# A fused RWKV-5 attention and ReLU-squared MLP kernel: q k^T in pairs of units, log w spread first, and another order of all steps

## The chip, the cores and the metric

The kernel runs on one core of a Trainium2 chip. Five engines work from their own in-order queues: TensorE (PE, matmuls and transposes), VectorE (DVE), ScalarE (ACT), GpSimd (POOL) and SyncE (SP); here POOL and SP mainly start DMA transfers. The metric is the device time of one launch in microseconds, lower is better; a time is the median of several runs.

## The reference

The first half is a linear-attention recurrence with a per-channel decay `w` and a bonus `u` for the current token; its output, laid out as 3072 tokens by 384 channels, goes through a two-layer MLP whose activation is the square of a ReLU.

```python
# r, k, v: (4, 8, 768, 48); w, u: (8, 48); moe_w_in: (384, 2048); moe_w_out: (2048, 384)
for t in range(S):
    cur = einsum('bhd,bhe->bhde', u[None] * kt, vt)
    y[:, :, t] = einsum('bhd,bhde->bhe', rt, state + cur)
    state = w[None, :, :, None] * state + einsum('bhd,bhe->bhde', kt, vt)
x = y.transpose(0, 2, 1, 3).reshape(B * S, H * D)
out = (maximum(x @ w_in, 0.0) ** 2) @ w_out
```

## The kernel before

The sequence is cut into 6 chunks of 128 tokens; a *unit* is one chunk of one of the 4 batches, so there are 24 units, numbered chunk by chunk. Within a chunk the recurrence becomes matrix products: r is scaled by powers of w and k by inverse powers (`scale`), both are turned so that channels lie on the partitions, and their product, masked to the strictly earlier tokens, weights v. What comes from earlier chunks goes through a state of 48 by 48 per head.

The code is a set of small step functions and one long string, `SCHEDULE`, which lists all steps in program order. Each engine executes its own steps in the order in which they stand there. The numbers behind `@` are the PSUM banks (there are 8) that a step takes. The steps that matter:

- `load:i:kt:SP` loads k (or r, v) of unit i with a DMA started by SP or POOL (192 KB); `win` and `wout` load a quarter of the two weight matrices, cast to bf16, started by POOL (384 KB each, line 274 and line 279).
- At the start, `spread_log` spreads log w over the partitions by a matmul (line 237) from a row that ACT has taken the logarithm of, and `power:0`, `power:1` (ACT, line 241) make the powers `wpos` for r and `wneg` for k from it. `columns` loads w and u again as columns, `spread_columns` transposes them (line 246), `copy_columns` copies them out, and `u_columns` and `end_columns` (POOL) prepare the bonus and the decay over a chunk. `fill` is a matmul whose result nobody reads; it keeps TensorE occupied.
- `scale:i:0` and `scale:i:1` (DVE, line 288) write the scaled r and k. For units 0 to 5 `turn` (TensorE, line 311) and `evict_rk` (ACT) turn them; for units 6 to 23 `turn_dma` does it with one transposing DMA on SP's queue.
- `rk` (DVE) multiplies turned r and k for the bonus. `at:i` (TensorE, line 328) is q k^T of the unit: 8 matmuls of contraction 64 into two banks; `mask:i:o` (DVE, line 336) masks one bank out to SBUF.
- `sums` (lines 344, 349) makes the bonus and the addition to the state, `diag_v`, `state_add`, `state_decay`, `state_cast` use it. `y_mm` (lines 387, 393) forms the attention output, `evict_y` writes it as bf16, and `x_turn`/`evict_x` (units 0 to 5) or `x_dma` (a transposing DMA on SP) turn it.
- `mm1:i:m:s` (line 431) is a piece of the first MLP layer for m units at once (one unit for units 0 to 7, two from 8 on), `relu` (ACT) and `square` (on ACT, line 448, or DVE, line 450, as its last number says) follow. `mm2:i:q` (line 457) is a quarter of the second layer of one unit, `evict_o` and `store` write out; the last unit's second layer is done in two halves (line 472).

Of the kernel before, what the change touches and what calls it, by code (L numbers as in the profile page):

```python
# [22 lines left out]
rk:1 at:1@6,7 cast_v:1 end_columns fill:256@5 at:0@0,1 mask:1:1 fill:256@5 load:6:kt:SP fill:256@5 sums:1@2 mask:1:0
2*fill:256@5 3*fill:256@7 diag_v:1 fill:256@7 load:3:rt:POOL y_mm:1@4 cast_v:0 load:6:rt:SP fill:256@7 scale:2:1
4*fill:256@7 evict_y:1 fill:256@7 win:2:0 4*fill:256@7 mask:0:0 x_turn:1@3 turn:2:1@5 load:4:kt:POOL evict_x:1
sums:0@7 scale:2:0 fill:256@4 evict_rk:2:1 fill:256@4 mask:0:1 fill:256@4 turn:2:0@6 win:3:0 cast_v:2 2*fill:256@3
diag_v:0 fill:256@5 evict_rk:2:0 y_mm:0@4 load:4:rt:POOL fill:256@5 scale:3:1 2*fill:256@5 at:2@0,3 load:8:rt:SP rk:2
mm1:1:1:1@5 mask:2:0 wout:0:0 load:5:kt:POOL sums:2@1 evict_y:0 turn:3:1@6 mask:2:1 x_turn:0@0 evict_rk:3:1
mm1:1:1:0@4 wout:1:0 scale:3:0 evict_x:0 load:4:vt:POOL y_mm:2@3 relu:1:1:1 diag_v:2 turn:3:0@6 mm1:0:1:1@0
evict_rk:3:0 evict_y:2 relu:1:1:0 state_add:1 at:3@5,3 cast_v:3 x_turn:2@6 mm1:0:1:0@4 rk:3 evict_x:2 mask:3:1  # L30
square:1:1:0:1 sums:3@2 mm1:0:1:2@6 mask:3:0 wout:2:0 load:7:rt:SP diag_v:3 mm1:2:1:1@3 relu:0:1:2 state_add:2
load:5:rt:POOL y_mm:3@5 square:0:1:2:1 mm1:2:1:0@6 scale:4:1 relu:0:1:0 mm1:2:1:2@1 evict_y:3 relu:2:1:0 state_add:0
turn:4:1@4 state_cast:1 mm1:1:1:2@5 wout:3:0 square:1:1:1:0 relu:0:1:1 x_turn:3@6 mm1:1:1:3@7 evict_x:3 load:5:vt:POOL
square:0:1:1:0 relu:1:1:2 mm1:0:1:3@0 relu:2:1:1 square:1:1:2:0 mm1:3:1:3@6 square:2:1:1:1 square:2:1:0:0 mm1:3:1:2@5
relu:2:1:2 square:0:1:0:0 mm1:3:1:0@3 evict_rk:4:1 scale:4:0 relu:3:1:3 mm2:2:0@1 relu:3:1:0 square:3:1:3:0 turn:4:0@4
state_cast:0 mm1:3:1:1@6 square:3:1:0:0 mm2:1:0@3 evict_rk:4:0 state_add:3 relu:3:1:2 mm2:1:1 scale:5:1 cast_v:4
square:3:1:2:0 relu:0:1:3 at:4@4,2 load:7:kt:SP mm2:3:0@5 state_cast:2 rk:4 mask:4:1 mm1:2:1:3@0 mask:4:0 sums:4@2
relu:2:1:3 mm2:2:1 scale:5:0 square:2:1:2:0 y_mm:4@4 load:8:kt:SP turn:5:1@0 diag_v:4 mm2:1:2 relu:1:1:3 scale:6:1
load:7:vt:SP square:2:1:3:1 mm2:2:2 evict_y:4 evict_rk:5:1 mm2:2:3 scale:6:0 relu:3:1:1 square:1:1:3:0 turn:5:0@7
turn_dma:6 square:0:1:3:1 mm2:0:0@4 state_add:4 cast_v:5 x_turn:4@0 evict_rk:5:0 mm2:1:3 load:6:vt:SP evict_x:4  # L40
at:5@6,2 state_cast:3 load:9:kt:SP mm1:4:1:1@7 mask:5:0 mm1:4:1:0@0 rk:5 load:9:rt:SP relu:4:1:1 scale:8:0 mm1:4:1:3@6
scale:7:0 relu:4:1:0 mask:5:1 mm1:4:1:2@7 square:3:1:1:1 scale:7:1 sums:5@0 relu:4:1:2 mm2:3:1 state_add:5 turn_dma:7
relu:4:1:3 mm2:3:2 square:4:1:1:1 diag_v:5 y_mm:5@2 scale:8:1 cast_v:7 load:8:vt:SP mm2:3:3 square:4:1:0:1 evict_y:5
turn_dma:8 state_decay:4 cast_v:6 at:6@7,6 mm2:4:0@0 square:4:1:3:1 mask:6:1 evict_o:3 load:11:rt:SP x_turn:5@2 rk:6
mm2:0:1 evict_o:1 square:4:1:2:0 load:10:rt:SP state_cast:4 sums:6@6 mask:6:0 mm2:0:2 evict_x:5 diag_v:6 mm2:4:1
state_add:6 y_mm:6@5 at:7@3,7 evict_y:6 mm1:5:1:3@2 mask:7:1 x_dma:6 mm1:5:1:2@6 rk:7 mask:7:0 mm1:5:1:0@5 relu:5:1:2
load:10:kt:SP scale:9:0 sums:7@7 load:9:vt:SP square:5:1:2:1 scale:9:1 y_mm:7@3 mm1:5:1:1@6 relu:5:1:0 state_add:7
turn_dma:9 relu:5:1:3 mm2:4:2 diag_v:7 cast_v:8 rk:8 mm2:0:3 relu:5:1:1 evict_y:7 square:5:1:0:1 state_decay:5
at:8@5,2 x_dma:7 sums:8@7 square:5:1:1:1 mask:8:0 mm1:6:1:0@6 evict_o:2 mask:8:1 mm1:6:1:1@3 load:11:kt:SP relu:6:1:0
diag_v:8 store:2:POOL load:12:kt:SP mm1:6:1:3@5 scale:10:0 store:1:POOL scale:11:0 y_mm:8@1 store:3:POOL relu:6:1:3  # L50
mm2:5:0@2 scale:10:1 square:6:1:0:1 square:5:1:3:0 mm2:5:1 turn_dma:10 relu:6:1:1 evict_y:8 mm1:6:1:2@6 cast_v:9 rk:9
evict_o:0 x_dma:8 at:9@5,3 state_cast:5 sums:9@1 mask:9:0 mm1:7:1:2@4 square:6:1:1:1 mask:9:1 load:11:vt:SP relu:6:1:2
# [5 lines left out]
load:13:rt:SP mm1:8:2:2@7 relu:8:2:1 mm1:8:2:3@1 cast_v:10 square:8:2:1:0 load:14:kt:SP relu:8:2:2 at:11@4,0 rk:11
cast_v:11 mm1:8:2:7@5 mask:11:1 relu:8:2:3 mm1:8:2:0@7 mask:11:0 square:8:2:3:1 sums:10@0 scale:12:0 relu:8:2:0
sums:11@1 y_mm:11@4 turn_dma:12 relu:8:2:7 diag_v:11 mm1:8:2:6@7 cast_v:12 diag_v:10 y_mm:10@5 evict_y:11 relu:8:2:6  # L60
mm2:6:3 square:8:2:0:0 square:8:2:2:1 x_dma:11 mm1:8:2:5@4 scale:13:1 evict_y:10 mm2:8:0@7 relu:8:2:5 load:15:rt:SP
scale:13:0 mm1:8:2:4@5 x_dma:10 square:8:2:5:1 scale:14:1 mm2:9:0@4 square:8:2:6:1 rk:12 square:8:2:7:1 scale:15:1
mm2:7:2 load:14:rt:SP state_add:11 relu:8:2:4 turn_dma:13 mm2:9:1 square:8:2:4:1 mm2:8:1 evict_o:6 load:15:vt:SP
cast_v:13 mm2:8:2 evict_o:5 store:6:POOL load:16:rt:SP sums:12@5 store:4:POOL at:12@1,3 diag_v:12 mm2:8:3 store:0:POOL
mask:12:1 mm1:10:2:1@2 mask:12:0 mm1:10:2:0@3 scale:15:0 relu:10:2:1 scale:14:0 mm1:10:2:3@1 relu:10:2:0 state_add:10
turn_dma:14 mm1:10:2:6@2 square:10:2:0:1 square:10:2:1:0 mm1:10:2:7@3 relu:10:2:3 state_add:12 turn_dma:15
mm1:10:2:2@0 relu:10:2:7 state_decay:9 relu:10:2:6 state_decay:10 at:13@1,5 state_decay:12 y_mm:12@3 relu:10:2:2
load:16:kt:SP rk:13 mm1:10:2:5@2 state_cast:9 evict_y:12 mm1:10:2:4@0 mask:13:1 x_dma:12 square:10:2:2:1 mask:13:0
mm2:7:3 relu:10:2:5 square:10:2:7:0 square:10:2:3:1 sums:13@3 load:14:vt:SP y_mm:13@5 relu:10:2:4 diag_v:13 mm2:11:0@1
state_cast:10 evict_y:13 mm2:10:0@2 scale:16:0 square:10:2:6:1 x_dma:13 mm2:11:1 rk:15 cast_v:15 state_add:13 mm2:9:2  # L70
evict_o:8 load:17:rt:SP square:10:2:4:1 rk:14 mm2:10:1 store:8:POOL state_decay:11 load:17:kt:SP square:10:2:5:1
store:5:POOL at:15@0,5 state_cast:12 load:16:vt:SP at:14@3,7 mm2:10:2 mask:14:1 load:19:rt:SP state_cast:11 mm2:11:2
mask:15:1 cast_v:14 evict_o:7 mm2:9:3 load:19:kt:SP state_decay:13 mask:15:0 sums:15@7 evict_o:9 scale:16:1
mm1:12:2:0@5 mask:14:0 mm1:12:2:1@6 turn_dma:16 sums:14@0 relu:12:2:1 y_mm:14@4 diag_v:14 mm1:12:2:5@3 evict_y:14
mm1:12:2:2@6 relu:12:2:5 scale:17:0 x_dma:14 mm1:12:2:4@4 relu:12:2:0 scale:17:1 diag_v:15 relu:12:2:2 y_mm:15@3
turn_dma:17 square:12:2:1:0 relu:12:2:4 mm2:11:3 cast_v:16 evict_y:15 mm2:10:3 square:12:2:2:1 square:12:2:0:0
# [465 lines left out]
```

## Time and profile before

| | |
|---|---|
| median of 3 runs | 176.25 us (174.26 to 177.11) |
| the profiled execution | 174.99 us |
| its span, first to last instruction | 173.1 us |
| granted TensorE clock | 1.000 |
| busy VectorE / ScalarE / GpSimd | 132.3 / 125.7 / 29.3 us |
| read from HBM, written | 20.45 MB, 4.72 MB |

The page gives busy time by engine, then 40 equal slices of the span with a digit for the busy share of each, the DMA queues (q1 carries what SP starts, q0 what POOL starts), the chain of work that ended last, and the costliest groups of instructions. A busy time of TensorE comes from modelled ends of pipelined matmuls, so the chain, which counts the time that a piece adds, is the better source for what a matmul costs. Under DMA issues, the last number of a row is the median time from issue to landing.

### The profile page before, as it was taken

What the parts mean: (1) busy time and instruction counts of PE and PEld (TensorE: products, weight loads), DVE (VectorE), ACT (ScalarE), POOL (GpSimd) and SP (SyncE); (2) the same over time, 40 slices, a digit from 0 to 9 for tenths busy, and PEclk for the clock granted to TensorE, in tenths of its full rate; (3) what the DMA queues carried; (4) which work ended last, traced back from release to release, by engine and by line L of the source; (5) the groups of instructions that cost most, each with busy time, mean ns of one, the idle gap of its engine ahead of it and who ended that gap; (6) DMA issues with size and microseconds to landing.
All of it is one profiled execution on the core that took longest, in us unless ns stands there. A gap on an engine that the chain in (4) does not pass through costs nothing.

```text
span 173.1 us, 4810 instructions
## 1 busy us (share of the span) xinstructions
PE 165.4 (96%) x1928; PEld 131.9 (76%) x1928; DVE 132.3 (76%) x289; ACT 125.7 (73%) x261; POOL 29.3 (17%) x61
## 2 busy tenths in 40 slices
...
DMA  5999999999996997999997997997969952122023
GB/s 110 198 207 227 215 240 236 245 172 115 205 172 125 200 207 145 200 202 118 254 183 172 209 160 154 193 157 223 225 100 229 263 140 45 27 68 91 4 99 128
DMA packets 95760, 28.83 MB, mean 167 GB/s; under 512 B 91689, under 2 KB 93738, under 8 KB 95738
## 3 DMA queue, kind: packets, MB, share of 16 engines
...
q8 instruction: 15, 0.25, 0.6%
...
HBM read 20.45 MB, written 4.72 MB: 145 GB/s over the span
## 4 chain that ended last, share of the span: by engine, by line
PE 70%; DMA 16%; DVE 4%; ACT 4%; POOL 2%; issue 1%; SPq 1%; DVEq 0%; ACTq 0%
PE bank L431 30%; PE bank L457 27%; DMA ldr<-in_r_dram 7%; DMA rkT<-rkw 6%; PE bank L328 3%; DMA xT<-yb 2%; ACT gr L439 2%; PE bank L387 2%; PE bank L393 2%; PE bank L472 2%; PE bank L349 2%; DVE rkw L288 2%; PE bank L344 1%; DVE g L450 1%; POOL wend_c L260 1%
## 5 line engine op out<-in xcount | busy, mean ns | idle before, releaser
L439 ACT ACTIVATE gr<-bank 128x512 f32<-128x512 f32 x96 | 54.5, 600 | 25.4 <-PE bank L431 24.8
L431 PE MATMUL bank<-xT,w_in_q 128*128 128x128 bf16 (+1 forms) x768 | 71.0, 246 | 0.5 <-DMA xT<-yb 0.5
L457 PE MATMUL bank<-w_out_q,g 128*128 128x384 bf16 x368 | 67.1, 326 | 0.0
L431 PEld LDWEIGHTS <-w_in_q 128*128 128x128 bf16 x768 | 63.6, 113 | 3.5 <-issue 0.7
L457 PEld LDWEIGHTS <-g 128*128 128x128 bf16 x368 | 34.3, 98 | 18.9
L336 DVE TENSOR_TENSOR am<-bank,smask 128x512 bf16<-128x512 f32 x48 | 31.6, 683 | 5.9 <-PE bank L328 5.0
L450 DVE TENSOR_TENSOR g<-gr 128x512 bf16<-128x512 f32 x41 | 27.3, 685 | 11.2 <-ACT gr L439 10.9
L448 ACT ACTIVATE g<-gr 128x512 bf16<-128x512 f32 x55 | 34.0, 635 | 0.6
...
L378 ACT CAST stb<-st 64x192 bf16<-64x192 f32 x40 | 14.0, 349 | 2.8 <-DVE st L372 2.5
L288 DVE TENSOR_TENSOR rkw<-ldk,wneg 128x384 bf16<-128x384 f32 x24 | 13.2, 552 | 3.3 <-ACT wneg L241 3.1
L358 DVE TENSOR_TENSOR dv<-vb,bank 128x384 f32<-128x384 bf16 x24 | 13.1, 548 | 2.5 <-PE bank L349 1.2
L402 DVE TENSOR_TENSOR yb<-bank,dv 128x384 bf16<-128x384 f32 x24 | 13.3, 554 | 1.9 <-PE bank L393 1.1
L288 DVE TENSOR_TENSOR rkw<-ldr,wpos 128x384 bf16<-128x384 f32 x24 | 12.9, 550 | 1.3 <-DMA ldr<-in_r_dram 1.3
L292 ACT CAST vb<-ldv 128x384 bf16<-128x384 f32 x24 | 12.4, 515 | 2.1 <-DMA ldv<-in_v_dram 2.0
L320 DVE TENSOR_TENSOR rk<-rkT 128x512 bf16<-128x512 bf16 x24 | 10.0, 418 | 4.4 <-DMA rkT<-rkw 2.7
L464 ACT COPY osb<-bank 128x384 f32<-128x384 f32 x23 | 10.7, 480 | 2.0 <-PE bank L457 1.9
L368 DVE TENSOR_TENSOR st<-bank,st 64x192 f32<-64x192 f32 x32 | 11.3, 352 | 0.3
L315 ACT COPY rkT<-bank 128x512 bf16<-128x512 bf16 x12 | 6.8, 588 | 4.8 <-PE bank L311 4.8
L233 PE MATMUL bank<-warm 128*128 128x256 bf16 (+1 forms) x50 | 9.1, 328 | 1.2 <-DVE warm L179 1.2
L328 PEld LDWEIGHTS <-rkT 64*128 64x128 bf16 x192 | 5.8, 94 | 5.2 <-issue 4.5
L328 PE MATMUL bank<-rkT 64*128 64x128 bf16 x192 | 9.1, 218 | 0.4 <-ACT rkT L315 0.2
...
## 6 DMA issues: line engine op xcount, KB each, us to landing
ldv<-in_v_dram SPq DMA_DIRECT2D x22, 192.0 KB, 4.5
ldk<-in_k_dram SPq DMA_DIRECT2D x21, 192.0 KB, 4.2
out_dram<-osb POOLq DMA_DIRECT2D x21, 192.0 KB, 3.3
ldr<-in_r_dram SPq DMA_DIRECT2D x19, 192.0 KB, 3.8
w_in_q<-in_moe_w_in_dram POOLq DMA_DIRECT2D x4, 384.0 KB, 7.3
w_out_q<-in_moe_w_out_dram POOLq DMA_DIRECT2D x4, 384.0 KB, 10.4
ldr<-in_r_dram POOLq DMA_DIRECT2D x5, 192.0 KB, 7.2
ldk<-in_k_dram POOLq DMA_DIRECT2D x3, 192.0 KB, 7.8
```

What stands on the lines that cost most here:

```text
L288: nc.vector.tensor_tensor(t["rkw"][:, x, :, :, :D], pair(src), pair(wx), ALU.mult)
L292: nc.scalar.copy(tiles[i]["vb"], tiles[i]["vt"])
L328: nc.tensor.matmul(out=t["at"][o][:, p, :], lhsT=t["rkT"][sl, 1, p, :], rhs=t["rkT"][sl, 0, p, :], start=True, stop=True,)
L336: nc.vector.tensor_tensor(am, t["at"][o], smask.unsqueeze(1).to_broadcast([C, HP, C]), ALU.mult)
L358: nc.vector.tensor_tensor(t["dv"], t["vb"], t["d"].unsqueeze(2).to_broadcast([C, H, D]), ALU.mult)
L378: nc.scalar.copy(stb[b][sl, :, o * D : (o + 1) * D], st32[b][sl])
L402: nc.vector.tensor_tensor(t["yb"], t["y"], t["dv"].rearrange("p h d -> p (h d)"), ALU.add)
L431: nc.tensor.matmul(out=t["h", s][:, a], lhsT=turned, rhs=chunks[c]["xT"][:, n, b : b + m, :], start=(n == 0), stop=(n == NK - 1),)
L439: nc.scalar.activation(t["gr", s], t["h", s], AF.Relu)
L448: nc.scalar.activation(g, x, AF.Square)
L450: nc.vector.tensor_tensor(g, x, x, ALU.mult)
L457: nc.tensor.matmul(out=t["o"], lhsT=chunks[units[i][0]]["g"][:, f, units[i][1], :], rhs=w_out_q[f // 4][:, f % 4, :], start=(f == 0), stop ...
```

## The change

Three things change, all in the order of the steps; the arithmetic stays the same.

1. A new step `ats:i` runs `at:i` and `at:i + 1` back to back, with four banks at once. For units 8 to 23 every q k^T is now such a pair.
2. At the start, `spread_log` comes behind 9 fills and ahead of `spread_columns`, which now stands behind the first four `turn` steps; before, it came behind 14 fills and was directly followed by `spread_columns`. `power:0` (for r) now precedes `power:1`.
3. The whole `SCHEDULE` is another one: other positions, banks, queues of some loads, and another choice of engine for the squares (50 of 96 on DVE where it was 41). The number of fills goes from 50 to 53.

```diff
+    def ats(i):
+        at(i)
+        at(i + 1)
+
     def mask(i, o):
...
-        at, cast_v, columns, copy_columns, diag_v, end_columns, evict_half, evict_o,
+        at, ats, cast_v, columns, copy_columns, diag_v, end_columns, evict_half, evict_o,
...
-load:1:kt:SP fill:256@7 load:0:kt:SP 2*fill:256@7 load:0:rt:SP 2*fill:256@7 load:1:rt:POOL 2*fill:256@7 load:1:vt:SP
-columns:0 2*fill:256@7 columns:1 fill:256@7 win:1:0 fill:256@7 load:2:kt:SP 2*fill:256@7 load:2:rt:POOL fill:128@7
-spread_log@0 load:0:vt:SP spread_columns@1 power:1 power:0 scale:1:1 2*fill:256@7 scale:0:0 turn:1:1@2 scale:0:1
...
-mm2:6:1 load:12:vt:SP mask:10:1 mm2:7:0@6 load:15:kt:SP state_decay:8 state_decay:6 state_cast:8 mm2:6:2 mask:10:0
...
+load:1:kt:SP fill:256@7 load:0:rt:SP 2*fill:256@7 load:0:kt:SP 2*fill:256@7 load:1:rt:POOL 2*fill:256@7 load:2:kt:SP
+2*fill:256@7 columns:0 columns:1 load:1:vt:POOL spread_log@0 load:2:vt:SP load:2:rt:POOL load:5:rt:SP fill:256@7
+power:0 win:0:0 2*fill:256@7 power:1 fill:256@7 scale:0:0 fill:256@7 load:0:vt:POOL fill:256@7 scale:1:1 2*fill:256@7
+turn:1:1@1 win:1:0 scale:0:1 turn:0:0@2 evict_rk:1:1 load:3:kt:POOL scale:1:0 turn:0:1@3 load:5:kt:SP evict_rk:0:0
...
+x_dma:8 mm1:7:1:2@6 relu:7:1:3 state_add:9 mm2:5:3 evict_o:4 square:7:1:1:0 cast_v:11 load:10:vt:SP mm2:7:0@1
+relu:7:1:2 state_decay:9 load:13:rt:SP rk:10 square:6:1:2:1 mm2:7:1 square:7:1:2:0 load:13:kt:SP evict_o:5 mm2:6:2
...
+square:7:1:3:1 scale:12:1 ats:10@0,5,3,2 turn_dma:12 mm1:8:2:0@6 mask:10:1 mm1:8:2:4@4 mask:11:1 relu:8:2:0
```

The queues at the start, in order. SP before: k1 k0 r0 v1 k2 v0 v2 v3 k6 r6 r8 r7 k7 k8 v7, then the transpose of unit 6; after: k1 r0 k0 k2 v2 r5 k5 r6 k6 k9 k7 k8 r7 r8 v6, then the same transpose. POOL before: r1 win 1, r2, `u_columns`, k3, win 0, `end_columns`, r3, win 2, k4, win 3, r4, wout 0, k5, wout 1, v4, wout 2, r5, wout 3, v5; after: r1 v1 r2, win 0, v0, win 1, k3, win 2, r3, `u_columns`, `end_columns`, win 3, v3, wout 0, r4, wout 1, k4, wout 2, v4, wout 3, v5.

More of the change, by code (lines that the diff above doesn't have):

```diff
@@ L23 @@
[L23 to L52, printed above, removed]
@@ L58 @@
[L58 to L76, printed above, removed]
-x_dma:15 mm1:12:2:7@5 square:12:2:5:1 state_add:15 mm1:12:2:3@6 square:12:2:4:0 load:18:kt:SP mm1:12:2:6@4 relu:12:2:3
@@ new lines @@
+turn:1:0@4 evict_rk:0:1 win:2:0 spread_columns@5 evict_rk:1:0 rk:0 load:3:rt:POOL cast_v:1 rk:1 at:1@6,7 copy_columns
+at:0@0,1 u_columns scale:2:0 fill:256@5 scale:2:1 fill:256@5 end_columns turn:2:0@2 fill:256@5 mask:0:0 turn:2:1@3
+evict_rk:2:0 sums:1@4 mask:0:1 evict_rk:2:1 3*fill:256@5 2*fill:256@2 mask:1:0 at:2@5,0 win:3:0 2*fill:256@3 mask:1:1
+2*fill:256@3 fill:256@6 cast_v:0 load:3:vt:POOL 2*fill:256@6 diag_v:1 fill:256@6 y_mm:1@2 y_mm:0@3 load:6:rt:SP
+sums:0@1 evict_y:1 wout:0:0 2*fill:256@7 rk:2 fill:256@7 load:4:rt:POOL x_turn:1@6 diag_v:0 2*fill:256@7 evict_x:1
@@ new lines @@
+2*fill:256@7 fill:256@2 evict_y:0 fill:256@2 wout:1:0 mm1:1:1:1@7 state_add:0 x_turn:0@2 load:4:kt:POOL mm1:1:1:0@6
+mask:2:1 evict_x:0 relu:1:1:1 state_add:1 mm1:0:1:0@3 relu:1:1:0 mm1:0:1:1@1 mask:2:0 square:1:1:1:1 scale:3:1
+relu:0:1:0 4*fill:256@7 square:1:1:0:0 fill:256@7 cast_v:2 3*fill:256@7 state_cast:1 fill:256@7 square:0:1:0:0
+sums:2@2 wout:2:0 y_mm:2@0 mm1:0:1:2@7 relu:0:1:1 diag_v:2 evict_y:2 mm1:1:1:2@4 load:4:vt:POOL load:6:kt:SP scale:3:0
+x_turn:2@6 turn:3:1@5 state_add:2 evict_x:2 turn:3:0@3 fill:256@0 evict_rk:3:1 fill:256@0 square:0:1:1:0 mm1:2:1:2@1
@@ new lines @@
+evict_rk:3:0 wout:3:0 mm1:2:1:0@0 relu:1:1:2 rk:3 relu:0:1:2 at:3@6,2 load:5:vt:POOL relu:2:1:0 mm1:2:1:1@5 mask:3:1
+cast_v:3 mm1:1:1:3@3 square:2:1:0:0 relu:2:1:1 mask:3:0 mm1:2:1:3@4 square:1:1:2:1 square:2:1:1:1 mm1:0:1:3@7
+scale:4:0 relu:2:1:2 mm2:1:0@0 relu:1:1:3 scale:5:0 sums:3@2 relu:0:1:3 y_mm:3@5 turn:4:0@6 diag_v:3 square:2:1:2:1
+mm2:0:0@1 square:0:1:2:1 evict_y:3 mm2:2:0@3 state_add:3 evict_rk:4:0 mm2:1:1 state_cast:0 scale:4:1 x_turn:3@7
+square:0:1:3:0 relu:2:1:3 mm2:0:1 evict_x:3 square:1:1:3:0 turn:4:1@5 mm2:2:1 evict_rk:4:1 load:9:kt:SP mm1:3:1:1@6
@@ new lines @@
+cast_v:4 rk:4 at:4@2,4 relu:3:1:1 load:7:kt:SP mm1:3:1:0@7 mask:4:1 square:2:1:3:1 mm2:1:2 mask:4:0 relu:3:1:0
+load:8:kt:SP square:3:1:1:0 turn:5:0@5 square:3:1:0:1 mm1:3:1:3@6 load:7:rt:SP scale:5:1 evict_rk:5:0 mm2:0:2
+relu:3:1:3 scale:6:0 sums:4@4 load:8:rt:SP cast_v:5 y_mm:4@2 diag_v:4 state_cast:2 mm2:2:2 scale:6:1 load:6:vt:SP
+square:3:1:3:1 turn:5:1@7 state_add:4 mm1:3:1:2@5 evict_rk:5:1 turn_dma:6 state_decay:4 mm2:3:0@6 relu:3:1:2 rk:5
+evict_y:4 mm2:3:1 square:3:1:2:1 scale:7:1 load:9:rt:SP state_cast:3 at:5@4,7 x_turn:4@5 mask:5:0 mm2:3:2 load:7:vt:SP
@@ new lines @@
+mm2:2:3 cast_v:7 rk:7 mm1:5:1:3@1 state_cast:5 turn_dma:9 state_add:6 square:4:1:1:1 at:7@4,7 mm1:5:1:1@6 mask:7:1
+relu:5:1:3 load:8:vt:SP evict_o:2 sums:7@0 mask:7:0 load:11:kt:SP mm2:4:1 relu:5:1:1 rk:8 load:11:rt:SP store:2:POOL
+relu:5:1:2 mm2:4:2 diag_v:7 store:3:POOL state_add:7 y_mm:7@1 store:0:POOL mm2:4:3 scale:10:1 store:1:POOL mm1:6:1:0@7
+evict_y:7 square:5:1:2:0 x_dma:7 mm1:6:1:1@3 relu:6:1:0 state_decay:7 mm2:5:0@4 square:5:1:1:0 square:6:1:0:1
+load:11:vt:SP square:5:1:3:1 ats:8@6,5,0,1 load:12:kt:SP relu:6:1:1 mm2:6:0@7 mask:8:0 mm1:6:1:3@3 rk:9 scale:10:0
@@ new lines @@
+state_decay:15 relu:14:2:7 load:20:rt:SP mm2:15:1 state_add:17 store:12:POOL load:21:kt:SP square:14:2:7:1 rk:18
+ats:18@5,1,6,4 store:11:POOL cast_v:19 load:22:kt:SP store:8:POOL mm2:14:2 state_cast:15 mask:18:1 mm2:15:2 mask:18:0
+sums:18@2 mask:19:0 sums:19@1 y_mm:18@5 mask:19:1 mm2:14:3 diag_v:18 mm1:16:2:1@6 diag_v:19 evict_y:18 mm1:16:2:6@4
+relu:16:2:1 state_add:18 x_dma:18 y_mm:19@5 relu:16:2:6 mm1:16:2:7@6 evict_y:19 mm1:16:2:0@2 scale:20:0 x_dma:19
+scale:21:0 mm1:16:2:4@4 relu:16:2:0 mm2:15:3 relu:16:2:7 load:23:kt:SP square:16:2:0:0 load:22:rt:SP mm1:16:2:3@5
@@ new lines @@
+scale:22:1 mm2:16:1 relu:18:2:0 load:23:vt:SP state_decay:19 mm1:18:2:2@0 square:18:2:3:0 relu:18:2:7 mm2:16:2
+relu:18:2:2 turn_dma:22 square:18:2:7:1 ats:20@6,4,2,3 state_cast:16 mm2:17:1 mask:20:1 square:18:2:4:1 mm2:17:2
+square:18:2:0:0 state_cast:17 mm1:18:2:6@0 mask:20:0 cast_v:20 mask:21:1 mm2:18:0@4 evict_o:14 rk:23 relu:18:2:6
+mm2:17:3 square:18:2:2:0 store:14:POOL cast_v:21 y_mm:20@6 mask:21:0 evict_o:17 store:13:POOL sums:20@3 mm2:18:1
+diag_v:20 store:15:POOL mm2:16:3 state_decay:18 rk:21 state_cast:18 mm2:19:0@7 evict_y:20 cast_v:23 sums:21@0 x_dma:20
```

96 lines of the change are left out of this document (54 added, 42 removed).

## The prediction

> **What bounds the kernel now.** I read the busy times first, then the waits of TensorE, then the chain of waits, in which every piece stands with the time that it adds.
>
> ```profile
> span 173.1 us, 4810 instructions
> ...
> PE 165.4 (96%) x1928; PEld 131.9 (76%) x1928; DVE 132.3 (76%) x289; ACT 125.7 (73%) x261; POOL 29.3 (17%) x61
> ...
> DMA  5999999999996997999997997997969952122023
> ```
>
> TensorE is the fullest engine, and the DMA engines are full until the 34th slice. The chain prices TensorE's steps:
>
> ```profile
> 20.71 0.67 PE bank L431 x12
> ...
> 23.03 0.68 PE bank L431 x12
> ...
> 38.79 0.22 PE bank L311 x4
> 39.01 0.65 PE bank L457 x4
> 39.66 0.17 PE bank L417 x3
> ...
> 49.68 0.20 PE bank L387 x8
> 49.88 0.17 PE bank L393 x4
> 50.05 0.33 PE bank L328 x8
> ...
> 60.51 0.19 PE bank L344 x4
> 60.70 0.19 PE bank L349 x4
> ...
> 107.50 0.55 PE bank L328 x16
> ...
> 150.91 3.27 PE bank L431 x30
> ...
> 167.22 2.65 PE bank L472 x32
> ...
> 169.90 0.29 DVE osb_last L483
> ```
>
> Summed over the kernel: first layer 32 pieces of 12 matmuls at 0.67 and 384 matmuls of two units at 3.27/30, 21.4 + 41.9; second layer 92 x 0.65 + 2.65 = 62.5; q k^T 16 x 0.33 + 4 x 0.55 = 7.5, since four of the eight pairs already stand together before (the x16 rows); `sums` 20 x 0.38 + 4 x 0.19 = 8.4; `y_mm` 24 x 0.20 + 20 x 0.17 = 8.2; 12 `turn` x 0.22 and 6 `x_turn` x 0.17, 3.6. That is 153.5 us of work that no order removes, apart from the pairs. TensorE ends at 169.87, so 16.4 us before that are fills and waiting, and 3.2 us of copy and store follow. A change of order can only win from these 19.6 us, and the last 3.2 keep their steps.
>
> Where do the 16.4 lie? I take as a mark the first use of quarter 2 of w_in, `mm1:0:1:2`, which begins at 23.03. The work in front of it is 8 `turn`, 4 q k^T, 4 `sums`, 3 `y_mm`, 3 `x_turn` and 4 first-layer pieces: 1.76 + 1.32 + 1.52 + 0.60 + 0.51 + 2.68 = 8.4 us. So 14.6 us are lost before the mark and 1.8 behind it. The start is the place; TensorE is nearly gapless afterwards.
>
> **The start.** What TensorE waits for there is data. The issues and the landing times (last number) of four transfers of POOL, r1, w_in 0, w_in 2 and the last w_out, and of one k that SP starts:
>
> ```profile
> 2.22 1.06 POOL L267 DMA_DIRECT2D ldr<-in_r_dram  x1
> 10.34 0.75 POOL L274 DMA_DIRECT2D w_in_q<-in_moe_w_in_dram  x1
> 13.97 0.76 POOL L274 DMA_DIRECT2D w_in_q<-in_moe_w_in_dram  x1
> 25.13 0.56 POOL L279 DMA_DIRECT2D w_out_q<-in_moe_w_out_dram  x1 [1.45 <-DMA w_in_q<-in_moe_w_in_dram]
> ...
> 11.82 2.01 SPq L267 DMA_DIRECT2D ldk<-in_k_dram  x1
> ...
> ldr<-in_r_dram POOLq DMA_DIRECT2D x1, 192.0 KB, 4.7
> w_in_q<-in_moe_w_in_dram POOLq DMA_DIRECT2D x1, 384.0 KB, 6.7
> w_in_q<-in_moe_w_in_dram POOLq DMA_DIRECT2D x1, 384.0 KB, 7.9
> w_out_q<-in_moe_w_out_dram POOLq DMA_DIRECT2D x1, 384.0 KB, 10.2
> ldk<-in_k_dram SPq DMA_DIRECT2D x1, 192.0 KB, 11.0
> ```
>
> Issue plus landing time: r1 is there at 6.9, w_in 0 at 17.0, w_in 2 at 21.9, the last w_out at 35.3. Between r1 and w_in 0 POOL's queue brought w_in 1, r2, k3 and w_in 0, 1152 KB in 10.1 us or 114 KB/us; it had little queued, since k3 is issued behind `u_columns`. Between w_in 0 and the last w_out it brought six loads and six quarters, 3456 KB in 18.3 us or 189 KB/us, with much queued; in that time SP's transfers starved (11.0 us for one k).
>
> After, POOL issues r1 v1 r2, w_in 0, v0, w_in 1, k3, w_in 2, r3 with nothing in between that waits; at 0.75 to 1.06 us each they are all issued by about 11, where w_in 2 alone was issued at 13.97 before. Behind r1 stand 1920 KB up to and with w_in 2. At 189 KB/us it lands at 17.1, at 114 at 23.7. I take the middle rate, 152, since POOL's queue is now deep, but SP has seven loads of its own queued beside it: 19.5.
>
> TensorE's own chain is the other bound. The first logarithm spread:
>
> ```profile
> 1.19 3.06 PE L233 MATMUL bank<-warm 128*128 128x256 bf16 x14 [1.19 <-DVE warm L179]
> ...
> 2.57 0.52 ACT L195 ACTIVATE lnw<-wrow 1x384 f32<-1x384 f32 x1
> ...
> 4.18 1.64 PE L237 MATMUL bank<-lnw,ones 1*128 1x384 f32 x2
> ...
> 16.94 0.86 PE L431 MATMUL bank<-xT,w_in_q 128*128 128x128 bf16 x12
> ...
> PE bank L246 <- DMA wu<-in_u_dram: 1.4, 1, 1.4
> ```
>
> Nine fills end at 1.19 + 9 x 3.06/14 = 3.2, and the logarithm is there at 3.1, so the spread starts 1.0 us earlier; and the 1.4 us wait for the columns no longer stands ahead of the first `turn` steps. The four `scale` steps gain less, since r and k must land: with r0 and k0 in exchanged places on SP I expect the fourth to end some 0.5 us earlier. The weights cover that gain: the first first-layer piece needs w_in 1, 1344 KB behind r1, so 15.7 by the middle rate (14.0 to 18.7).
>
> How early could TensorE itself be at the mark? Before, the first first-layer piece began at 16.94 with 3.6 us of work in front of it (6 `turn`, 3 q k^T, 2 `sums`, 2 `y_mm`, 1 `x_turn`), 14 fills at 0.22, 36 at 0.11 (3.27/30), the spread 1.6, the columns 0.5 and 1.2 at the front, 14.0 in all; 3.0 went to waits, 1.4 of them the wait for the columns. After, the mark has 7.1 us of work in front of it (two `turn`, one q k^T, one `sums` and one `x_turn` fewer than the 8.4), 9 fills at 0.22 and 42 at 0.11: with the spread, the columns, the front and the other 1.6 us of waits, 18.5. The later bound wins: the mark at 19.5, with 12.4 us lost in front of it instead of 14.6. That is **-2.2**, bounds -3.2 (18.5) and +2.0 (23.7). Two fills stand behind the mark: **+0.2**.
>
> Behind it the weights still set the pace: w_in 3 and each w_out come with one or two loads, 576 KB, 3.05 us at the full rate: 22.5, 25.6, 28.6, 31.7, 34.7. In front of their first uses lie 11.4, 13.4, 16.2, 20.2 and 28 us of work; with 12.4 lost these come at 23.8, 25.8, 28.6, 32.6 and 40. So the order meets the landings with nothing to spare for the first two w_out quarters, and a late one shows as a gap.
>
> **The pairs.** Two q k^T apart cost 0.66, together 0.55; only units 8/9, 10/11, 12/13 and 20/21 are new pairs: 4 x 0.11 is **-0.4**, bounds 0 and that.
>
> [...]
>
> **The steady part.** 1.8 us were lost behind the mark. Where a step takes a bank, I summed TensorE's work between the place of the step that empties the bank and that of the next that fills it, with the prices above: under 1.0 us in 83 of 225 hand-overs before, in 38 after. In proportion 1.8 becomes 0.8: **-1.0**; bounds -1.8 (none left) and +3 (one w_out a whole 3.05 us step late). Nine squares move to DVE:
>
> ```profile
> L450 DVE TENSOR_TENSOR g<-gr 128x512 bf16<-128x512 f32 x41 | 27.3, 685 | 11.2 <-ACT gr L439 10.9
> L448 ACT ACTIVATE g<-gr 128x512 bf16<-128x512 f32 x55 | 34.0, 635 | 0.6
> ```
>
> That is 6.2 us more on an engine with 41 us idle and 5.7 less on ACT: nothing, while DVE's order keeps the masks in time; without that cover, up to 6.2.
>
> Sum: -2.2 + 0.2 - 0.4 - 1.0 = -3.4, so a span of 169.7 and 171.6 for an execution like the profiled one (174.99, 1.9 outside the span). That one lies 1.3 below the median of the runs, 176.25; with the same difference the forecast is 172.9. About 2% (3.5 us) is what a measurement of this kernel can tell from no change, so the edges are 172.7 and 179.8, and the forecast lies on the first.
>
> **Rivals.** *The queues share evenly.* If POOL and SP are served as in the first 10 us, w_in 2 lands at 23.7 at worst; counted by bytes, with SP served as before, POOL has one load more in front of it than it had (r1 v1 r2 v0 k3 for r1 r2 k3 r3), 192 KB or 1.0 us: 22.9. The mark at 23.2 loses 16.1, +1.5 instead of -2.2: 176.6. For it: v1 and v0 join POOL's queue ahead of w_in 1 and 2, so the bytes in front grow; against it: the 189 KB/us. [...]
>
> *A pair waits for its second unit (slower).* The second transposing DMA of a pair has less work in front of the pair than a single unit needs to have: for unit 11 two first-layer and six second-layer pieces, 5.2 us; for the others of this kind 5.3 to 6.5 (9, 13, 15, 18, 21).
>
> ```profile
> L302 SPq DMA_TRANSPOSE rkT<-rkw x18: 1232/1520/2848, 38.7 to 136.6; - x18
> ...
> DMA to landing us min/median/max: 3.6/4.9/5.9
> ...
> PE bank L431 <- DMA xT<-yb: 0.5, 1, 0.5
> PE bank L328 <- ACT rkT L315: 0.2, 1, 0.2
> ```
>
> A landing takes 4.9, up to 5.9, and SP's queue can still be issuing a transpose (1.5) when its turn comes: 6.4 to 7.4. That decides from 5.2 on: a stall of 0.1 to 2.2 us in each of eight pairs, about 1 us each, and TensorE cannot go round it. +8 on 172.9 is 181. Against it: the least cover before was as short (5.3, unit 18), and TensorE's waits (the last two rows) name nothing over 0.5 us. For it: some loads have little cover now too, 3.8 us for r and k of unit 17 and r of 18.
>
> *The change does not do what it says* for half its pairs, which were pairs already; that is in the sum.
>
> **How the numbers follow.** Forecast 0.58. With all its bounds of gain it gives 176.25 - 3.2 + 0.2 - 0.4 - 1.8 = 171.0, and the median of a few runs can lie 1 us lower: 170.0; with the bound of a late landing it reaches 175. I give 0.42 to under 172.7 and 0.16 above, as the two bounds on the start are not equally far. Even sharing 0.17: 174.5 to 180, 0.15 of it within 2% and 0.02 slower. Late pairs 0.25: 0.23 slower, 0.02 within. Together faster 0.42, within 0.33, slower 0.25. The range 170.0 to 181.0 leaves out the upper half of the last case, some 0.12, and little below.
>
> **What would show it.** In the new profile: the first w_in 2 piece near 19.5 (23 would mean even sharing); no L246 wait ahead of the first turns; eight x16 rows of 0.55 for L328; waits of L328 on the transposes at most 0.5 us each. I am wrong if w_in or w_out pieces wait longer than 2 us, or if TensorE's gaps lie at the pairs.

## The result, and the profile after

The changed kernel takes 173.41 us, the median of 20 runs (172.49 to 175.16); the kernel before, run beside it 20 times, takes 176.49 (174.26 to 178.82). The ratio is 0.9876, with an interval of 0.9845 to 0.9908: about 1.2% faster, inside the 2% that counted as no change. The ratio is taken over the executions within 1.5% of the fastest of their kernel, which is why it is nearer to 1 than that of the two medians (0.983). The forecast was 172.9, the range 170.0 to 181.0. The profiled execution took 173.05 us with a span of 171.3, 1.8 less than the span before.

The page of the changed kernel, with the same lines as before:

```profile
span 171.3 us, 4810 instructions
...
PE 164.8 (96%) x1931; PEld 132.1 (77%) x1931; DVE 138.0 (81%) x298; ACT 120.8 (71%) x252; POOL 30.5 (18%) x62
...
PEclk9987999999999999999999999999999999999999
```

TensorE is as full as it was. The granted clock dips in the third and fourth slices, which it did not before (its mean was 1.000). TensorE's waits (total, times, longest):

```profile
PE bank L311 <- DVE rkw L288: 1.6, 1, 1.6
PE bank L233 <- DVE warm L179: 1.2, 1, 1.2
PE bank L328 <- ACT rkT L315: 0.8, 1, 0.8
```

The wait for the columns (L246) and the one for `xT` are gone; the wait of a `turn` for a scaled r or k, 0.9 before (at 20.31), is 1.6 now and lies earlier. Where, TensorE's timeline shows (start, time, what, and in brackets the idle time before it and its releaser):

```profile
4.80 1.89 PE L233 MATMUL bank<-warm 128*128 128x256 bf16 x8
6.60 1.74 PE L311 MATMUL bank<-identb,rkw 128*128 128x128 bf16 x16
...
9.35 0.62 PE L328 MATMUL bank<-rkT 64*128 64x128 bf16 x16 [0.80 <-ACT rkT L315]
9.91 0.39 PE L233 MATMUL bank<-warm 128*128 128x256 bf16 x2
11.89 0.61 PE L311 MATMUL bank<-identb,rkw 128*128 128x128 bf16 x4 [1.60 <-DVE rkw L288]
...
13.37 1.27 PE L233 MATMUL bank<-warm 128*128 128x256 bf16 x5
...
15.02 1.05 PE L233 MATMUL bank<-warm 128*128 128x256 bf16 x8
...
17.88 0.83 PE L435 MATMUL bank<-xT,w_in_q 128*128 128x128 bf16 x12
...
22.24 1.51 PE L435 MATMUL bank<-xT,w_in_q 128*128 128x128 bf16 x24
```

The mark of the prediction, the first use of quarter 2 of w_in, comes at 22.24 (23.03 before, 19.5 forecast), and the first first-layer piece at 17.88 (16.94 before). The idle stretch lies in front of `turn:2:0`. The rows also tell the clock: four matmuls of a `turn` take 0.61 at 11.89 but 0.40 at full speed; eight fills take 1.05 at full speed (15.02) but 1.89 at 4.80, and five take 1.27 at 13.37. So TensorE ran at half speed up to about 8 us and once more around 13. VectorE says what was late:

```profile
11.28 0.56 DVE L288 TENSOR_TENSOR rkw<-ldr,wpos 128x384 bf16<-128x384 f32 x1 [1.45 <-DMA ldr<-in_r_dram]
11.75 0.55 DVE L288 TENSOR_TENSOR rkw<-ldk,wneg 128x384 bf16<-128x384 f32 x1
12.23 2.48 DVE L340 TENSOR_TENSOR am<-bank,smask 128x512 bf16<-128x512 f32 x4
```

r of unit 2 was late, and behind its `scale` stand, in VectorE's order, the other `scale` and the four masks of units 0 and 1, on which the first attention outputs depend. r2 is no later than it was: in the kernel before it was issued at 4.03 and landed 7.2 later. But there masks stood ahead of its `scale` on VectorE, the first two at 11.51:

```profile
11.51 1.29 DVE L336 TENSOR_TENSOR am<-bank,smask 128x512 bf16<-128x512 f32 x2
...
14.71 0.55 DVE L288 TENSOR_TENSOR rkw<-ldr,wpos 128x384 bf16<-128x384 f32 x1
```

POOL's timeline and, below it, the DMA issues (last number: issue to landing) of that r and of w_in 2:

```profile
4.17 0.88 POOL L267 DMA_DIRECT2D ldr<-in_r_dram  x1
...
8.34 0.75 POOL L274 DMA_DIRECT2D w_in_q<-in_moe_w_in_dram  x1
```

```profile
ldr<-in_r_dram POOLq DMA_DIRECT2D x1, 192.0 KB, 7.1
w_in_q<-in_moe_w_in_dram POOLq DMA_DIRECT2D x1, 384.0 KB, 11.6
```

r landed at 11.25, w_in 2 at 19.9. The weights were on time (19.5 was forecast), but TensorE reached their first use 2.3 us after they were there.

The granted clock by stretches of 2 us (length, busy time of each engine, and after POOL the clock):

```profile
10.00:12.00 2.00, 0.40 (x4) 0.12 (x4) 0.72 (x2) 0.00 (x0) 1.56 (x8) 0.86 1.22 188
12.00:14.00 2.00, 2.00 (x20) 1.75 (x20) 2.00 (x4) 1.17 (x2) 1.74 (x6) 0.50 1.19 238
14.00:16.00 2.00, 2.00 (x23) 1.39 (x22) 1.16 (x3) 0.51 (x1) 2.00 (x3) 0.78 1.18 240
```

A mean of 0.86 is 0.56 us at half speed, 0.78 is 0.88 us, so the clock was halved from about 11.4 to 14.9, 3.4 us.

Last, the chain of waits around one pair and at the end:

```profile
58.05 0.65 PE bank L461 x4
58.70 0.55 PE bank L328 x16
59.25 0.76 PE bank L461 x4
...
165.83 2.65 PE bank L476 x32
...
168.51 0.29 DVE osb_last L487
```

All eight x16 rows behind 58 us are 0.55, and no wait of TensorE on a transposed rk is named anywhere.

### The profile page after: what moved, and what is told of

Same layout as the page of the kernel before. It is cut to its first block, busy times and chain, and to the rows that moved or that the text cites. A ratio compares the mean times of both kernels' runs of the same rounds, so it can differ in the third digit from the quotient of the medians.

```text
span 171.3 us, 4810 instructions
## 1 busy us (share of the span) xinstructions
PE 164.8 (96%) x1931; PEld 132.1 (77%) x1931; DVE 138.0 (81%) x298; ACT 120.8 (71%) x252; POOL 30.5 (18%) x62
## 4 chain that ended last, share of the span: by engine, by line
PE 87%; DVE 5%; DMA 4%; POOL 2%; issue 1%; POOLq 0%; DVEq 0%
PE bank L461 35%; PE bank L435 35%; DMA ldr<-in_r_dram 4%; PE bank L328 4%; PE bank L391 3%; PE bank L353 2%; PE bank L397 2%; PE bank L476 2%; PE bank L233 1%; PE bank L311 1%; PE bank L348 1%; DVE yb L406 1%; DVE am L340 1%; DVE st L370 1%; PE bank L421 1%
## 5 line engine op out<-in xcount | busy, mean ns | idle before, releaser
L443 ACT ACTIVATE gr<-bank 128x512 f32<-128x512 f32 x96 | 53.8, 603 | 27.8 <-PE bank L435 24.4
L454 DVE TENSOR_TENSOR g<-gr 128x512 bf16<-128x512 f32 x50 | 33.0, 686 | 6.5 <-ACT gr L443 6.4
L340 DVE TENSOR_TENSOR am<-bank,smask 128x512 bf16<-128x512 f32 x48 | 30.8, 684 | 3.5 <-PE bank L328 3.2
L452 ACT ACTIVATE g<-gr 128x512 bf16<-128x512 f32 x46 | 28.2, 633 | 0.5
L288 DVE TENSOR_TENSOR rkw<-ldk,wneg 128x384 bf16<-128x384 f32 x24 | 13.1, 552 | 0.6 <-DMA ldk<-in_k_dram 0.5
L233 PE MATMUL bank<-warm 128*128 128x256 bf16 x53 | 10.0, 336 | 1.2 <-DVE warm L179 1.2
L328 PE MATMUL bank<-rkT 64*128 64x128 bf16 x192 | 8.1, 220 | 0.8 <-ACT rkT L315 0.8
```

What stands on the lines that cost most here:

```text
L288: nc.vector.tensor_tensor(t["rkw"][:, x, :, :, :D], pair(src), pair(wx), ALU.mult)
L328: nc.tensor.matmul(out=t["at"][o][:, p, :], lhsT=t["rkT"][sl, 1, p, :], rhs=t["rkT"][sl, 0, p, :], start=True, stop=True,)
L443: nc.scalar.activation(t["gr", s], t["h", s], AF.Relu)
L452: nc.scalar.activation(g, x, AF.Square)
L454: nc.vector.tensor_tensor(g, x, x, ALU.mult)
```

## The experiments

Each kernel was timed against the kernel before on the same chip; a number in brackets behind a ratio is its 95% interval. The experiments ran on four chips, so kernels are compared by their ratios, and one profiled execution stands for each kernel. Three explanations stood against each other at first. A: r2's landing, which VectorE's order puts ahead of the masks, sets the start, and the place of the logarithm is covered by it. The rival: the logarithm's place is what gained. Beside them the question what the pairs are worth. Later came C: what counts is when TensorE gets its full clock, and idle stretches decide that. In some kernels two lines were added ahead of the steps, so a line number in their rows is 2 higher (L437 is the first layer, L330 q k^T); kernels made from the one before have its numbers (L431 is the first layer).

**r2 first.** Two loads of POOL change places.

```diff
-columns:1 load:1:vt:POOL spread_log@0 load:2:vt:SP load:2:rt:POOL load:5:rt:SP
+columns:1 load:2:rt:POOL spread_log@0 load:2:vt:SP load:1:vt:POOL load:5:rt:SP
```

> The changed kernel with one exchange on POOL's queue: r of unit 2 is loaded ahead of v of unit 1. Theory A (r2's landing at 11.25 us holds scale:2:0, which stands ahead of the masks of units 0 and 1 on DVE): r2 lands near 9.3, the 1.6 us wait of the turn of unit 2 goes, the granted clock stays at 1.00 there, the first first-layer piece comes at about 16.5 instead of 17.9 and the median falls by 1 to 1.5 us. Theory B (the weights set the start: w_in 1 at 16.2, w_in 2 at 19.9): the wait goes but the time stays within 0.4 us.

172.19 us, ratio 0.9829 [0.9776, 0.9882]. TensorE's timeline and, below it, its wait:

```profile
10.52 0.40 PE L313 MATMUL bank<-identb,rkw 128*128 128x128 bf16 x4
...
20.63 1.51 PE L437 MATMUL bank<-xT,w_in_q 128*128 128x128 bf16 x24
```

```profile
PE bank L437 <- DMA xT<-yb: 1.7, 1, 1.7
```

The `turn` of unit 2 comes 1.4 us earlier, without an idle stretch and at full speed (0.40), and the mark 1.6 earlier. So r2 did hold the start. But the profiled span is 171.3 again: at 83.8 us a first-layer piece now waits 1.7 for the transposed output of unit 10, so this execution, 1.1 above the median, gave the gain back in the middle. The ratio is 0.0047 (0.8 us) under that of the changed kernel, and the intervals overlap.

**Late logarithm.** The spread goes behind 14 fills, with `spread_columns` right behind it, as in the kernel before.

```diff
-load:1:vt:POOL spread_log@0 load:2:vt:SP load:2:rt:POOL load:5:rt:SP fill power:0 win:0:0 2*fill power:1 fill scale:0:0 fill
+load:1:vt:POOL load:2:vt:SP load:2:rt:POOL load:5:rt:SP fill win:0:0 4*fill spread_log@0 spread_columns@5 power:0 power:1 scale:0:0
...
-win:2:0 spread_columns@5 evict_rk:1:0
+win:2:0 evict_rk:1:0
```

> The changed kernel with the spread of log w behind 14 fills and directly followed by the spread of the columns, as before. Theory A: the early spread is hidden behind r2's landing, so the time stays within 0.4 us, although the first turn of r and k comes 1 to 1.5 us later. Rival: the early spread is what brought the gain; then the median rises by 1 us or more.

174.37 us, 0.9933 [0.9894, 0.9972], by the ratios about 1 us slower than the changed kernel (0.9933 - 0.9876 is 0.0057 of 175) and 0.6 slower than its control below (0.9900); both intervals overlap. A's 0.4 was too small, if anything. TensorE's timeline:

```profile
11.01 1.03 PE L330 MATMUL bank<-rkT 64*128 64x128 bf16 x16 [0.86 <-ACT rkT L317]
...
15.08 0.61 PE L330 MATMUL bank<-rkT 64*128 64x128 bf16 x8
15.62 1.05 PE L235 MATMUL bank<-warm 128*128 128x256 bf16 x8
```

Two units' q k^T takes 1.03 instead of 0.62: TensorE ran at half speed until 15.6. The mark came at 22.85, 0.6 later than in the changed kernel.

**Both.** r2 first and the late logarithm, edits as above.

> Both of these edits together. Theory A: with r2 early, the late spread is no longer hidden: 0.5 to 1.2 us slower than r2 first alone, and still faster than or equal to the changed kernel. If B holds, this one equals the changed kernel within 0.4 us.

174.09 us, 0.9933 [0.9898, 0.9968]; half speed until 15.9, the mark at 23.00. With r2 first, the late logarithm costs 0.0104 or 1.8 us, and the intervals (this one and that of r2 first alone) lie apart. With the late logarithm, an early r2 gains nothing: TensorE reaches the `turn` of unit 2 at 12.46 without a wait, and at 12.38, without one too, with r2 late (in the changed kernel it lands at 11.25). Both executions were at half speed there, which first pointed to the clock; that TensorE's chain is simply later (its first `turn` at 8.31 where it was at 6.60) is not told apart from it.

**Pairs taken apart.** Each `ats` becomes two `at`, with the next step of TensorE between them.

```diff
-ats:8@6,5,0,1 load:12:kt:SP relu:6:1:1 mm2:6:0@7 mask:8:0
+at:8@6,5 load:12:kt:SP relu:6:1:1 mm2:6:0@7 at:9@0,1 mask:8:0
...
```

> The changed kernel with each of the eight pairs of q k^T taken apart by the TensorE step that followed it (0.65 us). By the rows of the profile (0.55 for a pair, 0.33 for one alone) it is 8 x 0.11 = 0.9 us slower, plus what the masks of the second unit lose by coming 0.65 us later (0 to 0.5 a pair). Rival (two halves of a unit run together in any case and a pair brings nothing): within 0.4 us.

175.6 us, 1.0023 [1.0000, 1.0047]: the whole gain of the change is gone. The chain where the pair of the changed kernel stood at 58.70:

```profile
59.02 0.65 PE bank L463 x4
59.67 0.33 PE bank L330 x8
60.00 0.76 PE bank L463 x4
60.76 0.33 PE bank L330 x8
61.09 1.46 PE bank L437 x24
```

The block that follows a q k^T is 0.11 to 0.12 dearer than its like elsewhere (0.76 for 0.65; 24 first-layer matmuls 1.46, in the changed kernel 1.34 behind a second-layer piece). Apart there are two such blocks, together one. So parting a pair costs 0.11 in the q k^T itself and 0.11 in the work behind it, 0.22. For eight pairs that is 1.8. (The chain goes by ends; by starts, in the timeline, the same 0.1 lies ahead of the q k^T: in the kernel before, 12 second-layer matmuls take 2.04 from 63.78 to the q k^T at 65.82, where the chain has 1.95. The sum of 0.22 does not depend on it.) The profiled span is 2.8 longer; 1.2 of that lies ahead of the mark (23.44), where this execution was at half speed once more (eight fills in 1.89), and 1.6 behind it.

**The changed kernel again**, as a control for the next two.

> The changed kernel once more, on the chip of the other three, as the mark they are measured from: a ratio of 0.985 to 0.991 to the kernel before.

173.93 us, 0.9900 [0.9861, 0.9939]. Its timeline differs from that of the first profile, though nothing in the kernel does:

```profile
9.35 1.04 PE L328 MATMUL bank<-rkT 64*128 64x128 bf16 x16 [0.55 <-ACT rkT L315]
...
14.90 1.89 PE L233 MATMUL bank<-warm 128*128 128x256 bf16 x8
...
23.05 1.51 PE L435 MATMUL bank<-xT,w_in_q 128*128 128x128 bf16 x24
```

The same 16 matmuls took 0.62 then and 1.04 now, the eight fills 1.05 and 1.89. Half speed lasts until 16.9 without a break, and the mark comes 0.8 later.

**The idle stretch filled.** 13 fills go ahead of `turn:2:0`; r2 stays as late as it is.

```diff
-end_columns turn:2:0@2
+end_columns 13*fill:256@5 turn:2:0@2
```

> The changed kernel with 13 more fills (1.4 us of TensorE time) ahead of the turn of unit 2, so that TensorE does not fall idle while r2 is on its way; r2 lands as late as before. Theory C (the loss at the start is the granted clock, which drops to half after the idle stretch, from 11.5 to 14.9 us): the clock stays at 1.00, the 8 fills behind q k^T of unit 2 take 0.9 us and end 1 us earlier, and the median falls by 0.5 to 1.1 us. Theory A alone (r2's landing holds the masks on DVE): within 0.4 us.

172.30 us, 0.9853 [0.9807, 0.9899].

```profile
9.91 1.81 PE L233 MATMUL bank<-warm 128*128 128x256 bf16 x15
11.96 0.40 PE L311 MATMUL bank<-identb,rkw 128*128 128x128 bf16 x4 [0.24 <-DVE rkw L288]
...
13.91 1.05 PE L233 MATMUL bank<-warm 128*128 128x256 bf16 x8
...
21.24 1.51 PE L435 MATMUL bank<-xT,w_in_q 128*128 128x128 bf16 x24
```

With r2 just as late, the `turn` runs at full speed and the mark comes 1.0 before that of the first profile and 1.8 before that of the control. More work that nobody reads, and an earlier mark: that speaks for C. The ratio is 0.0047 (0.8 us) under the control's, but the intervals overlap. With r2 first, which takes the wait away as well, the mark was at 20.63: of the 1.6 us that this gained on the first profile, 1.0 come without an earlier r2.

**r2 first, and unit 10's transpose early.** The first experiment with the wait at 83.8 taken away by earlier steps.

```diff
-x_dma:11 square:8:2:4:1 square:8:2:1:0 mm1:8:2:6@0 evict_y:10 mm1:8:2:5@3 load:12:vt:SP relu:8:2:6 square:8:2:2:0 x_dma:10
+x_dma:11 square:8:2:4:1 evict_y:10 square:8:2:1:0 mm1:8:2:6@0 mm1:8:2:5@3 x_dma:10 load:12:vt:SP relu:8:2:6 square:8:2:2:0
```

> r2 loaded ahead of v1, and in addition the output of unit 10 is written by DVE ahead of a square, and its transposing DMA stands ahead of the load of v12 on SP's queue. If the stall of 1.7 us in front of the first layer of units 10 and 11, which the profile with r2 first showed, ate part of the gain, it goes, and the median lies 0.4 to 1.2 us below that of r2 first alone (ratio 0.976 to 0.981). Rival (the stall was one execution's): 0.982 to 0.984.

172.48 us, 0.9842 [0.9796, 0.9888], no better than with r2 first alone, as the rival of this experiment had it. The wait is gone and the profiled span is 170.2, but this execution ran at half speed until 13.1. Whether the wait was in all executions of the first kernel was not tried.

**The kernel before with its logarithm first.** The spread behind 9 fills, the columns behind the first four turns.

```diff
-columns:0 2*fill:256@7 columns:1
+columns:0 2*fill:256@7 spread_log@0 columns:1
...
-fill:128@7 spread_log@0 load:0:vt:SP spread_columns@1 power:1
+fill:128@7 load:0:vt:SP power:1
...
-evict_rk:1:1 copy_columns scale:1:0 turn:0:1@4 u_columns turn:1:0@5 evict_rk:0:1 load:2:vt:SP load:3:kt:POOL
+evict_rk:1:1 scale:1:0 turn:0:1@4 turn:1:0@5 spread_columns@1 copy_columns evict_rk:0:1 load:2:vt:SP load:3:kt:POOL u_columns
```

> The kernel before with the early spread of log w alone: behind 9 fills, the columns spread behind the first four turns. Theory: its start is held by r3, which lands at 19.65 and whose scaled form TensorE waits for until 20.31, so the early spread alone gives nothing: within 0.4 us of before. Rival: it gives 1 us or more (ratio 0.994 or less).

175.31 us, 0.9991 [0.9957, 1.0026]: nothing. The profiled execution was at half speed until 13.8, and its first first-layer piece began at 17.83 (16.94 before). Whether the early logarithm would gain here with an earlier clock is not shown. In the middle, this kernel's timeline has waits of TensorE where the new order has none:

```profile
81.92 0.40 PE L328 MATMUL bank<-rkT 64*128 64x128 bf16 x8 [0.50 <-DVE st L368]
...
87.74 0.40 PE L328 MATMUL bank<-rkT 64*128 64x128 bf16 x8 [0.73 <-DMA rkT<-rkw]
...
98.31 0.93 PE L431 MATMUL bank<-xT,w_in_q 128*128 128x256 bf16 x7 [0.80 <-DMA xT<-yb]
```

That is 2.0 us, and the last two are for transposing DMAs. The steps there are those of the kernel before, whose own profile names only the last of the three, with 0.53.

**The kernel before with two transposes early.** Unit 12's rk and unit 10's output are turned before the loads that stand ahead of them on SP's queue.

```diff
-scale:12:1 mm2:5:3 load:13:vt:SP
+scale:12:1 scale:12:0 turn_dma:12 mm2:5:3 load:13:vt:SP
...
-scale:13:1 evict_y:10 mm2:8:0@7 relu:8:2:5 load:15:rt:SP scale:13:0 mm1:8:2:4@5 x_dma:10
+evict_y:10 scale:13:1 mm2:8:0@7 relu:8:2:5 x_dma:10 load:15:rt:SP scale:13:0 mm1:8:2:4@5
```

> The kernel before with two transposing DMAs issued earlier: scaled r of unit 12 and its transpose some 3 us earlier, ahead of three loads on SP's queue, and the output of unit 10 ahead of the scaling of k13 and of the load of r15. Theory D (the time lost behind the start was waits for transposes, 0.34 at 81.7 and 0.70 at 97.2 us of the profile before): 0.5 to 0.9 us less, ratio 0.995 to 0.997, and these two waits are gone from the trace. Theory E (it was lost at bank hand-overs with too little work between): within 0.3 us, and the waits stay or move.

176.78 us, 1.0012 [0.9968, 1.0055]: a miss. The profiled execution was 1.3 us above that median, so its rows are only a hint: the wait at 97 is gone, but VectorE waited 4.2 us in all for r, and TensorE once for 1.9 on a line released by VectorE. The loads that were pushed back may have lost their cover.

**No fills.** The 34 fills between `turn:1:0` and `sums:2` of the changed kernel are dropped.

```diff
-scale:2:0 fill:256@5 scale:2:1 fill:256@5 end_columns turn:2:0@2 fill:256@5 mask:0:0
+scale:2:0 scale:2:1 end_columns turn:2:0@2 mask:0:0
...
```

> The changed kernel without the 34 fills between the last of the first four turns and the sums of unit 2. Theory C (the granted clock stays at half until TensorE has been busy long enough): half speed until 17 us or later, the first use of w_in 2 at 22.5 to 24, the median 0 to 1.5 us above the changed kernel. Rival (these fills only stand in the way of late work): the first use at 20 to 21, 0.8 to 1.5 us faster than the changed kernel.

173.87 us, 0.9894 [0.9860, 0.9928], as the changed kernel. The fills put no cost on the whole and bring no gain; in the profiled execution, again above its median, half speed lasted until 20.8, and the mark still came at 22.16. So half speed is no loss where it only takes the place of fills (34 at 0.11 are 3.7 us).

**A start in another order.** On top of r2 first and the early transpose: three fills where TensorE waits for ScalarE's copies of rk, the cast of v2 ahead of POOL's v3, a state addition behind a mask, and the nine fills ahead of `sums:2` dropped.

```diff
-rk:1 at:1@6,7
+rk:1 3*fill:256@6 at:1@6,7
...
-cast_v:0 load:3:vt:POOL
+cast_v:0 cast_v:2 load:3:vt:POOL
...
-relu:1:1:1 state_add:1 mm1:0:1:0@3 relu:1:1:0 mm1:0:1:1@1 mask:2:0 square:1:1:1:1
+relu:1:1:1 mm1:0:1:0@3 relu:1:1:0 mm1:0:1:1@1 mask:2:0 state_add:1 square:1:1:1:1
...
```

> r2 ahead of v1 and the output of unit 10 early, as in the run before, and the rest of the start in another order: three fills ahead of the first q k^T, v2 cast right behind v0, the second mask of unit 2 ahead of a state update, and the 9 fills ahead of the sums of unit 2 left out, so that the first use of w_in 2 can follow its landing (19.9 us in the profile after). Theory: that use comes at 19.9 to 20.2 instead of 20.8, and the ratio is 0.974 to 0.981. Rival (another landing then holds TensorE, the first w_out at 25.5): 0.982 to 0.986.

171.48 us (171.29 to 174.53), 0.9762 [0.9713, 0.9811]: the fastest kernel of the study, about 2.4% under the kernel before; its interval lies wholly under that of the changed kernel. The profiled span is 169.5.

```profile
20.55 1.53 PE L435 MATMUL bank<-xT,w_in_q 128*128 128x128 bf16 x24 [0.75 <-DMA w_in_q<-in_moe_w_in_dram]
```

Here at last the mark waits for w_in 2, as the prediction had it. Which of the four edits brought how much was not tried.

**w_in 2 ahead of k3**, on top of that.

```diff
-load:3:kt:POOL scale:1:0 turn:0:1@3 load:5:kt:SP evict_rk:0:0 turn:1:0@4 evict_rk:0:1 win:2:0
+win:2:0 scale:1:0 turn:0:1@3 load:5:kt:SP evict_rk:0:0 turn:1:0@4 evict_rk:0:1 load:3:kt:POOL
...
-scale:3:1 relu:0:1:0 square:1:1:0:0 state_cast:1 square:0:1:0:0 sums:2@2 wout:2:0 y_mm:2@0 mm1:0:1:2@7 relu:0:1:1 diag_v:2 evict_y:2
+relu:0:1:0 square:1:1:0:0 state_cast:1 square:0:1:0:0 sums:2@2 wout:2:0 y_mm:2@0 mm1:0:1:2@7 relu:0:1:1 diag_v:2 evict_y:2 scale:3:1
```

> The kernel with the start in another order, and w_in 2 loaded ahead of k3 on POOL's queue (k3 is scaled behind the output of unit 2 then). Theory: its start is now held by w_in 2, for which TensorE waited 0.8 us until 20.55; with k3 (192 KB, 1.0 us at 189 KB/us) behind it, w_in 2 lands 0.8 to 1.1 us earlier, the wait goes and the ratio falls by 0.003 to 0.006, to 0.970 to 0.974. Rival (the queue is not what sets this landing, or the next landing holds TensorE): 0.975 to 0.979.

172.62 us, 0.9824 [0.9776, 0.9871], slower than the kernel that it was made from, if anything. The wait for the weights is gone, yet the mark came at 20.44, hardly earlier, and a wait of the first `x_turn` steps behind it appeared:

```profile
PE bank L421 <- DVE yb L406: 0.8, 1, 0.8
```

This execution had half speed until 13.6 where the other had it until 9.6. Whether the clock or VectorE's new order cost the time stays open.

## Why the prediction was right, and where it was wrong

The total was right: 173.41 for 172.9, in the range. What came, no change by the 2%, had a chance of 0.33, and faster than that had 0.42; by the ratio the change is worth 2.2 us (0.0124 of 176.5) where 3.4 were forecast. The parts were not right. On the profiled pair:

| term | forecast | found |
|---|---|---|
| start, to the mark | -2.2 | +0.5: 15.1 us lost (22.24 less 7.1 of work) for 14.6 |
| pairs | -0.4 | -0.9: four new pairs at 0.22 |
| steady part with two more fills | -0.8 | -1.1: 1.8 lost behind the mark before, 0.7 after (168.48 - 22.24, less 146.4 - 0.9 of work) |
| behind TensorE's end | 0 | -0.4 |
| sum | -3.4 | -1.9 |

The medians differ by 3.1, more than the profiled pair, and in the control by 1.0% or 1.8 us. The profiled execution of the kernel before was 1.5 under the median of its 20 runs and that of the changed one 0.4, while the forecast took one difference, 1.3, for both: some of the good agreement is luck.

One price in the sum of 153.5 is misread. The 0.38 for `sums` comes from rows right behind a q k^T (60.51); elsewhere the kernel before has 0.27:

```profile
73.31 0.08 PE bank L344 x4
73.39 0.19 PE bank L349 x4
```

That is 0.11 too much for each of 24, or 2.6, and the 0.11 that each of the 20 single or paired q k^T costs beside itself, 2.2, was left out. Both errors are in both kernels and nearly cancel, so the differences in the table hold to about 0.1.

**The start is the step that failed.** "TensorE's own chain is the other bound", 18.5, and "The later bound wins: the mark at 19.5". The landings were right: w_in 2 at 19.9 for 19.5, so the middle rate held and *even sharing* (22.9) fell. But TensorE's own chain was at 22.24. My sum kept "the other 1.6 us of waits" and full-speed prices. It missed two things. First, VectorE's in-order queue: `scale:2:0` waits for r2 (11.25), and in the new order four masks stand behind it. Second, the clock: TensorE ran at half speed up to about 8 us, idled for 0.8 and 1.6 us between 8.5 and 11.9, and ran at half speed for another 3.4. Of the 3.7 us between 18.5 and 22.24, the waits make 0.8 (2.4 for 1.6), the eight fills ahead of the turns 0.9 (1.80 for 0.88), the 16 matmuls of the first four turns 0.8 (1.67 for 0.88), and the second half-speed stretch about 1.5 (3.0 of its 3.4 us were work, at half pace); smaller terms take back 0.3. In the kernel before, too, "the other 1.6 us of waits" were nearly all half speed: beside the columns, TensorE's waits name only 0.2 before 16.94, but the same 16 matmuls and eight fills around them ran at half pace there:

```profile
7.86 1.91 PE L311 MATMUL bank<-identb,rkw 128*128 128x128 bf16 x16
```

That r2 holds the start is shown by the first experiment, and that it does so partly through the clock is supported by the filled stretch and by the mean clocks of all executions (below). "The mark at 19.5 set by the weights" became nearly true, at 20.55, only in the reordered start.

**"The weights cover that gain"** of the early logarithm is wrong once r2 comes first: there the late logarithm cost 1.8 us. In the changed kernel it cost 0.6 to 1.0, which the intervals do not set apart from nothing, and in the kernel before the early one brought nothing. How much of the cost is the clock is open.

**The pairs** were priced by the q k^T alone (0.66 for 0.55). The work next to it pays as much again, so 0.22 a pair.

**The steady part**: the size was about right, by another mechanism. I counted hand-overs of banks; the waits that traces name in the order before (0.53 in its own profile, 2.0 in that of its logarithm-first variant) are mostly for transposing DMAs, behind loads in SP's queue. Moving two of them in the kernel before gained nothing, so what in the new order removes them is open. That hand-overs play no part is not shown.

**The late second unit of a pair** (181) did not come: eight rows of 0.55, no wait. **The squares** on VectorE cost nothing that shows, as forecast: 5.7 us more on VectorE (138.0), 4.9 less on ScalarE (120.8). **The 0.4 behind TensorE's end** was not forecast, and its cause was not tried.
